# H3 convolution layers interleaved with ReLU MLPs on one core: a different early order, paired hidden buffers, two chunks kept in SBUF, and 70 extra small matmuls

## The chip, the core and the metric

The kernel runs on one core of a Trainium2 chip. Its engines are TensorE (PE in the profile; PEld is its weight load), VectorE (DVE), ScalarE (ACT), GpSimd (POOL) and SyncE (SP, which here issues nearly all transfers). Each works through its own list of instructions in the order in which the program put them, and waits where an operand isn't there. The metric is the device time of one execution in microseconds.

## What is computed

The input x (1 x 2048 x 640, float32) goes through four layers in turn, each with a residual: a gated long convolution (A), an MLP (B), and both again with the same weights.

```python
x = q
for _ in range(2):
    x = x + layernorm(x) * (longconv(shift(k) * v, ssm_k) + shift(k) * v * ssm_D)   # A
    x = x + relu(layernorm(x) @ w1) @ w2                                            # B
```

The convolution doesn't depend on x: it is one array Y (2048 x 640), used twice. shift is a causal convolution over 4 taps, longconv a causal one over all 2048 positions, per channel. w1 is 640 x 1728, w2 is 1728 x 640.

## The kernel before, in words

The 2048 rows are cut into 8 chunks of 256, and each chunk into two halves of 128 rows. The convolution works in a transformed domain: `transform` (line 356) makes the spectra of a chunk's inputs (`at`) and of its filter piece (`gt`), `products` (543) multiplies and adds them over all earlier chunks on VectorE (lines 583 to 587), transforms back and writes Y. Spectra that later chunks need go out to DRAM in `spills` (533) and come back through `get` (570) into a ring of four buffers, `ag`.

The MLP is made of float16 pairs. A float32 value is split into a high part and a low remainder, and a product is three matmuls: high by high, high by low, low by high. To split the weights they are first scaled by a power of two worked out from their norms. `norms` (672) loads the 14 tiles of w1 and then the 14 of w2 (320 KB each, line 682) and sums their squares on TensorE into `pw0` and `pw1` (line 689, five matmuls for each tile). A VectorE instruction takes the diagonal (694), a small matmul sums it (`pn`, 696), and a short chain of one-element instructions on VectorE and ScalarE (697 to 700) gives the scale `wsc`. `wsplit` (708) then makes of each of the 28 tiles a high part on ScalarE (716) and a low part on VectorE (717); tile 6 of w1 gets two small copies more (722).

`prep` (817) normalises a half or a whole chunk and brings it to TensorE's layout, `xT`, as a high and a low part. For the very first half this is done with transposes on TensorE (889) and copies by ScalarE (895) and VectorE (893); all others use DMA transposes (882). The first half's chain is: mean on VectorE (848), centred copy `xc` (850), squares on ScalarE (849), root (851), reciprocal `rstdB` on VectorE (852), high part `xh` on ScalarE (853), low part `xl` on VectorE (854).

`main` (898) is the MLP of one half or chunk. It goes through seven blocks of 256 hidden units in the order 0, 1, 2, 3, 6, 4, 5 (JS, line 30). `mm1` (994) gives a block's hidden values in one of two PSUM buffers `h`; ScalarE takes the ReLU as high part `hh` (1054, 1059), VectorE the remainder `hl` (1055, 1060), which frees the PSUM buffer; `mm2` (977) multiplies `hh` and `hl` with w2 into the sums `o` and `oc`. The rings of `hh` and `hl` hold two buffers each (NH). Block 6 is a half block and has one more matmul of its own (1067), which waits for a copy by ScalarE (`tb`, 1058). The first two chunks are worked on half by half (mains 0 to 7), the others whole. The last mains use a scheme with seven products for eight (line 942).

The order of all this isn't written out. Every operation is recorded with an engine, an assumed cost, what it reads and writes, and a class of urgency; `Plan.order` (129) then plays a list scheduler over them and fixes the order of each engine's list. For transfers it assumes a rate (DBW, line 49). So a change of one assumed number moves instructions on every engine. 50 small matmuls without use at the program's start (line 1162) are part of the kernel before.

Of the kernel before, what the change touches and what calls it, by code (L numbers as in the profile page):

```python
# [13 lines left out]
F16 = mybir.dt.float16  # L14
# [7 lines left out]
P = 128  # L22
S = 2048
# [3 lines left out]
NC = S // C  # L27
# [11 lines left out]
NSPIN = 50  # L39
BM = 1.7  # L40
CLS = (0, 1, 2.2, 2, 2.5, 3)
DDP = -6.5
CP = (-7, -6, -4.9)
WLAG = 3
POOLMOD = 5
CRIT, SLACK = -1, 0.6
PEOUT = 0.35
SAFE = 1.5
DBW, DLAT = 310e3, 1.9
LATE_DOWN = 0.0  # L50

# [10 lines left out]
AADD, RADD = (), ()  # L62
GADD, SADD = 4, 4
WINO = ((7, 0), (6, 1), (7, 1))
ONPOOL = ()

# [28 lines left out]
class Plan:  # L95
# [5 lines left out]
    def op(self, eng, cost, fn, reads=(), writes=(), prio=0, nbytes=0, late=0.0):  # L101
        o = Op()
        o.late = late
        o.eng, o.cost, o.fn, o.seq, o.nbytes = eng, cost, fn, len(self.ops), nbytes
        o.prio = (prio, o.seq)
        deps, o.new, o.outs = set(), [], []
        for t in reads:
# [21 lines left out]
    def order(self):  # L129
# [27 lines left out]
        while n < len(self.ops):  # L157
# [27 lines left out]
            for e in engs:  # L185
# [23 lines left out]
                if best.nbytes:  # L209
                    dma = max(dma, now + DLAT) + best.nbytes / DBW  # L210
                    end = dma + 1.1
# [26 lines left out]
def tile_h3_mlp(ctx: ExitStack, tc: tile.TileContext, q, kT, vT, shk, hF, hR, dD, w1, w2, cM, cG, out):  # L238
# [21 lines left out]
    def pe(cost, fn, reads, writes, prio, late=0.0):  # L260
        plan.op("PE", cost, fn, reads, writes, prio, late=late)
# [271 lines left out]
    def spills(u, at, gt, pr_):  # L533
        for i, (c, t) in enumerate(u):
            if c < NC - 2 or c == NC - 2 == u[-1][0]:
                dma(3072, lambda i=i, c=c, t=t: SP.dma_start(G_d[c][t].t, gt[:, i].rearrange("p a b c -> p (a b c)")), [gt], [G_d[c][t]], max(pr_, SPILL))
                dma(3072, lambda i=i, c=c, t=t: SP.dma_start(A_d[c][t].t, at[:, i].rearrange("p a b -> p (a b)")), [at], [A_d[c][t]], max(pr_, SPILL))

    Ysb = {}

    gate = Tile(None, [], F32, "gate")

    def products(u, at, gt, after):
# [18 lines left out]
        else:  # L562
            for i, (a, t) in enumerate(u):
                macs += [(i, c, a - c, t) for c in range(a + 1)]
        tl = {}
        for i, (c, t) in enumerate(u):
            tl["A", c, t] = (at, lambda i=i: at[:, i].rearrange("p a b -> p (a b)"))
            tl["G", c, t] = (gt, lambda i=i: gt[:, i].rearrange("p a b c -> p (a b c)"))

        def get(k, c, t):  # L570
# [101 lines left out]
    def norms():  # L672
# [3 lines left out]
        for k, e in ((0, 9), (1, 13)):  # L676
# [23 lines left out]
            dve(1, lambda pw=pw, sc=sc, e=e: DVE.tensor_scalar(sc.t, pw.t, -1.0, float((254 + e) << 23), op0=ALU.mult, op1=ALU.add), [pw], [sc], URGENT)  # L700
            out_.append((pw, sc))
        (p0, s0), (p1, s1) = out_
        inv = keep(const, [P, 1], "winv")
# [194 lines left out]
    def main(n, a, layer, S, xTS):  # L898
# [26 lines left out]
        fin = (a, layer) == (NC - 1, 1)  # L925
        plain = (NFP - 1, JS[-1]) if fin else (NFP - 1,)

# [94 lines left out]
        def second(j, *x):  # L1022
            if len(x) == 4:
                wprod(j, *x)
            else:
                wplain(j, *x)

        prev = None
# [169 lines left out]
    xTs = [prep(0, 0, (0,), CRIT)]  # L1198
    xTs.append(prep(0, 0, (1,), BACK))
    wsplit()  # L1200
    xT = xTs[0]
    cGs = csplit(cGt, 4, True, [WT[JS[-1], 1, 1]])
    for n, (a, l, S) in enumerate(order):
        nxt = xTs[1] if n == 0 else xT
        if n + 1 < len(order):
            na, nl, nS = order[n + 1]
            if n == 0 or nl == 0 and nS == (1,):
                pass
            elif nl == 0:
                conv_to(na)  # L1210
# [94 lines left out]
```

## Time and profile before

| what | value |
|---|---|
| time, median of 3 | 859.57 us (859.12 to 860.65) |
| the profiled execution | 859.22 us |
| its span, first to last instruction | 857.4 us |
| TensorE busy | 839.9 us, 7738 matmuls |
| VectorE busy | 743.4 us |
| ScalarE busy | 482.9 us |
| mean granted clock of TensorE | 0.995 |
| moved by DMA | 181.18 MB |

The 1.8 us between the span and the execution's time are outside the program's instructions. A row of the timeline holds the start, the duration, engine, line, operation, output and inputs of an instruction or of several equal ones, and in brackets how long its engine stood idle before it and what ended that. A row of the view by stretches holds the stretch, its length, then the busy time of PE, PEld, DVE, ACT and POOL with the number of instructions, the granted clock, the share of the DMA engines and GB/s.

### The profile page before, as it was taken

Reading aid. Unit: us, or ns where it says so; the run is one execution under the profiler, and the core shown is the slowest. Engines: PE = TensorE matmul, PEld = TensorE weight load, DVE = VectorE, ACT = ScalarE, POOL = GpSimd, SP = SyncE. Lnnn points to the kernel's source line nnn. Section 1 sums busy time; section 2 is a strip of 40 time slices with the busy share of each in tenths; the row PEclk is TensorE's granted clock in tenths of the full one; section 3 lists DMA queues with packets and bytes.
Section 4 is the critical chain, followed back from the end, with each engine's and each line's share of the span. In section 5 each row is a group of like instructions: output and inputs, shape, how many; then the busy total and the mean of one; then the engine's idle time right before and its main releaser. Section 6 shows DMA issues by size and latency. Waiting matters only on the chain.

```text
span 857.4 us, 19580 instructions
## 1 busy us (share of the span) xinstructions
PE 839.9 (98%) x7738; PEld 661.2 (77%) x7738; DVE 743.4 (87%) x1367; ACT 482.9 (56%) x1121; POOL 46.2 (5%) x57
## 2 busy tenths in 40 slices
PE   8789999999999999999999999999999999999997
PEld 8767788788878777777777777778777777888886
DVE  7999999999999999999999999999887758655543
ACT  6687586546586366738448283735416265737331
POOL 1000000000011001101011000011000000000000
PEclk9899999999999999999999999999999999999999
DMA  9886868998999969989898878597987663110200
GB/s 326 317 279 243 276 198 279 275 311 276 288 254 288 339 168 271 202 254 242 213 244 245 224 212 185 175 268 229 239 283 248 152 196 93 32 33 1 45 19 31
DMA packets 134989, 181.18 MB, mean 211 GB/s; under 512 B 50673, under 2 KB 87281, under 8 KB 134898
## 3 DMA queue, kind: packets, MB, share of 16 engines
q1 hardware_dynamic: 126578, 169.46, 64.0%
q0 software_dynamic: 8320, 10.49, 8.5%
q8 instruction: 60, 0.98, 0.5%
q14 instruction: 31, 0.25, 0.1%
HBM read 123.61 MB, written 35.65 MB: 186 GB/s over the span
## 4 chain that ended last, share of the span: by engine, by line
PE 85%; DVE 8%; ACT 4%; issue 1%; DMA 1%; SPq 0%; DVEq 0%; ACTq 0%
PE h L1015 12%; PE h L1018 12%; PE h L1016 12%; PE o L987 8%; PE o L988 8%; PE o L990 8%; PE o L942 7%; PE oc L987 2%; PE oc L988 2%; PE oc L990 2%; PE pg L466 1%; ACT w L716 1%; PE pq L609 1%; PE hb L1015 1%; PE hb L1016 1%
## 5 line engine op out<-in xcount | busy, mean ns | idle before, releaser
L1015 PE MATMUL h<-xT,w 128*128 128x256 f16 (+1 forms) x1290 | 301.5, 252 | 2.1 <-DVE hl L1060 1.9
L1018 PE MATMUL h<-xT,w 128*128 128x256 f16 (+1 forms) x1290 | 301.2, 251 | 0.0
L1016 PE MATMUL h<-xT,w 128*128 128x256 f16 (+1 forms) x1290 | 301.2, 251 | 0.0
L1016 PEld LDWEIGHTS <-w 128*128 128x128 f16 x1390 | 136.0, 98 | 14.1 <-issue 3.6
L1015 PEld LDWEIGHTS <-w 128*128 128x128 f16 x1390 | 136.1, 98 | 10.5
L988 PE MATMUL o<-w,hh 128*128 128x512 f16 x364 | 137.9, 379 | 0.4 <-DVE w L717 0.4
L987 PE MATMUL o<-w,hh 128*128 128x512 f16 x364 | 138.1, 379 | 0.0
L587 DVE TENSOR_TENSOR pacc<-pacc,pd 128x768 f32<-128x768 f32 x140 | 133.2, 952 | 0.8
L1018 PEld LDWEIGHTS <-w 128*128 128x128 f16 x1290 | 126.2, 98 | 8.9
L990 PE MATMUL o<-w,hl 128*128 128x512 f16 x338 | 128.1, 379 | 0.0
L1054 ACT ACTIVATE hh<-h 128x512 f16<-128x512 f32 (+1 forms) x103 | 50.6, 491 | 120.9 <-PE h L1018 119.7
L987 PEld LDWEIGHTS <-hh 128*128 128x128 f16 x728 | 71.2, 98 | 45.3 <-issue 1.0
L988 PEld LDWEIGHTS <-hh 128*128 128x128 f16 x728 | 71.3, 98 | 45.2
L990 PEld LDWEIGHTS <-hl 128*128 128x128 f16 x676 | 66.1, 98 | 40.5 <-issue 0.9
L586 DVE TENSOR_TENSOR pd<-Ax,Gx 128x768 f32<-128x768 f32 x87 | 81.7, 951 | 3.3 <-DMA Gx<-G 3.2
L987 PE MATMUL oc<-w,hh 128*128 128x128 f16 x364 | 79.7, 219 | 0.0
L988 PE MATMUL oc<-w,hh 128*128 128x128 f16 x364 | 79.7, 219 | 0.0
L990 PE MATMUL oc<-w,hl 128*128 128x128 f16 x338 | 74.0, 219 | 0.0
L1055 DVE SCALAR_TENSOR_TENSOR hl<-h,hh 128x512 f16<-128x512 f32 (+1 forms) x103 | 57.9, 562 | 12.0 <-ACT hh L1054 11.8
L389 ACT ACTIVATE tp<-kt,shs 128x256 f32<-128x256 f32 (+1 forms) x78 | 43.4, 574 | 20.3 <-DVE acc L426 20.3
L586 DVE TENSOR_TENSOR pd<-at,Gx 128x768 f32<-128x768 f32 x44 | 41.2, 952 | 0.5 <-DMA Gx<-G 0.5
L407 POOL DMA_DIRECT2D gs<-hr x20 | 19.0, 948 | 359.5 <-ACT tp L389 189.5
(225 smaller groups left out, 1556.4 us busy)
## 6 DMA issues: line engine op xcount, KB each, us to landing
Ax<-A SPq DMA_DIRECT2D x91, 384.0 KB, 4.5
Gx<-G SPq DMA_DIRECT2D x91, 384.0 KB, 4.6
G<-gt SPq DMA_DIRECT2D x32, 384.0 KB, 4.2
A<-at SPq DMA_DIRECT2D x32, 384.0 KB, 5.1
y<-Y SPq DMA_DIRECT2D x30, 320.0 KB, 4.2
ws<-in_w SPq DMA_DIRECT2D x28, 320.0 KB, 6.6
x<-in_q SPq DMA_DIRECT2D x16, 320.0 KB, 4.9
out_dram<-x SPq DMA_DIRECT2D x16, 320.0 KB, 2.7
```

What stands on the lines that cost most here:

```text
L389: ACT.activation(o[:, i : i + m], kview(i, m, j), AF.Copy, scale=shs[:, t, j : j + 1])
L586: ew(f"mac{j % POOLMOD}", 768, lambda e, pd=pd, av=av, gv=gv: e.tensor_mul(pd.t, av(), gv()), [ax, gx], [pd], pr_)
L587: dve(768, lambda i=i, pd=pd: DVE.tensor_add(acc[:, i], acc[:, i], pd.t), [acc, pd], [acc], pr_)
L942: PE.matmul(b[:, c : c + w], x, y[:, z : z + w], start=done[i] == 1, stop=done[i] == total[i])
L987: PE.matmul(z, hh[:, c], wh[:, d], start=(j == JS[0] and i == 0 and (h == 0 or s == S[0])), stop=False)
L988: PE.matmul(z, hh[:, c], wl[:, d], start=False, stop=end and tail)
L990: PE.matmul(z, hl[:, c], wh[:, d], start=False, stop=end)
L1015: PE.matmul(p[:, z], wh, xv(t, 0), start=b, stop=False)
L1016: PE.matmul(p[:, z], wh, xv(t, 1), start=False, stop=tail and e)
L1018: PE.matmul(p[:, z], wl, xv(t, 0), start=False, stop=e)
L1054: act(2 * R, lambda p=p, hh=hh: ACT.activation(hh.t, p.t, AF.Relu), [p], [hh], URGENT)
L1055: dve(2 * R, lambda p=p, hh=hh, hl=hl: DVE.scalar_tensor_tensor(hl.t, p.t, 0.0, hh.t, op0=ALU.max, op1=ALU.subtract), [p, hh], [hl], URGENT)
```

## The change

- The planner assumes 385 GB/s for transfers in its first 45 us and 310 GB/s after that, in place of 310 throughout.
- For the mains of a half chunk, `hh` and `hl` of a block share one buffer, and the blocks take it in turn from the ring that was for `hh` and the one that was for `hl`. A buffer is wide enough for both, so four blocks can be held at a time in place of two. The class `Part` stands for one of the two.
- 70 small matmuls (identity by identity, 128 x 128, float16) are recorded behind the norm of w1, with the lowest urgency. They read `s2`, that norm's sums, so that none starts ahead of it.
- The spectra of chunk 6 for the last two blocks of channels stay in their buffers for the products of chunk 7 (`held`) and are no longer stored and loaded again.
- Three edits name new constants that change no instruction: BK has the value of BM; EARLY asks for a main of a chunk ahead of the last, of the first layer, in the seven-product list, and there is none; and `conv_to(NC)` reaches the same units as `conv_to(7)`.

The diff, cut to its core (a plus is the changed kernel):

```diff
+NWARM = 70
+DBW0, FIRST = 385e3, 45
+PAIRED = 1
...
-                    dma = max(dma, now + DLAT) + best.nbytes / DBW
+                    dma = max(dma, now + DLAT) + best.nbytes / (DBW0 if now < FIRST else DBW)
...
-            if c < NC - 2 or c == NC - 2 == u[-1][0]:
+            if c < NC - 2:
...
-        tl = {}
+        tl = dict(held)
...
+        if u[0][0] == NC - 2 == u[-1][0]:
+            held.update(tl)
...
+            if k == 0 and NWARM:
+                spin2 = T(ps, "h", 2, [P, 512], "spin2", stream=2)
+                for _ in range(NWARM):
+                    pe(0.057, lambda spin2=spin2: PE.matmul(spin2[:, 0:P], ident16.t, ident16.t, start=True, stop=True), [ident16, s2], [spin2], IDLE)
...
-                hh = T(mlp, "hh", NH, [P, 2 * R], f"hh{n}_{j}", F16, stream=sm)
-                hl = T(mlp, "hl", NH, [P, 2 * R], f"hl{n}_{j}", F16, stream=sm)
+                if len(S) == 1 and PAIRED:
+                    both_parts = T(mlp, ("hh", "hl")[JS.index(j) % 2], NH, [P, 2, 2 * R], f"hh{n}_{j}", F16, stream=sm)
+                    hh, hl = (Part(both_parts, k) for k in range(2))
+                else:
+                    hh = T(mlp, "hh", NH, [P, 2 * R], f"hh{n}_{j}", F16, stream=sm)
+                    hl = T(mlp, "hl", NH, [P, 2 * R], f"hl{n}_{j}", F16, stream=sm)
```

What the planner makes of it, in the order of the changed program's lists up to the end of main 0:

- SP: the first tiles of w1 go among the last inputs of chunk 0: one ahead of `kt`, one ahead of `vt`, two ahead of `hf`, where before two stood behind `vt` and none earlier. The last tile of w2 waits for no engine any more, only for its place in the queue. The DMA transposes for main 1 come eleven places later. From the end of chunk 6 on, four stores and four loads of 384 KB are gone.
- PE: `pn0` stands behind 45 of the 70 matmuls into `pw1` (ten before). The other 25, in fives, have 52 small matmuls among and behind them: 3, 10, 10, 10 and 19; then `pn1`, 18 small ones, both groups of transposes, and only then the first product of main 0. Before, the transposes and the first product stood among the last 25. Main 0 then runs `mm1` of blocks 0 to 3, and from there on takes `mm1` of block 6 (both halves) and of block 4, further ahead of `mm2` than before, and three halves of `mm1` of main 1 (one before) ahead of the last product of main 0.
- DVE: the diagonal of `pw1` stands ahead of `rstdB`, and the first low part of a weight behind both (before, that low part stood ahead of `rstdB` and the diagonal eleven places behind it).
- ACT: the ReLU of block 6 stands ahead of the splits of block 4 of w1 (before, behind those, behind two splits of w2 and behind both of block 5).

More of the change, by code (lines that the diff above doesn't have):

```diff
@@ L39 @@
 NSPIN = 50
-BM = 1.7
+BM, BK = 1.7, 1.7
 CLS = (0, 1, 2.2, 2, 2.5, 3)
@@ L63 @@
 GADD, SADD = 4, 4
+PAIRED = 1
 WINO = ((7, 0), (6, 1), (7, 1))
+EARLY = 3
 ONPOOL = ()
@@ L105, in op @@
         o.prio = (prio, o.seq)
+        reads, writes = ([getattr(t, "tile", t) for t in x] for x in (reads, writes))
         deps, o.new, o.outs = set(), [], []
@@ L539, in tile_h3_mlp @@
     Ysb = {}
+    held = {}
     gate = Tile(None, [], F32, "gate")
@@ L925, in main @@
         fin = (a, layer) == (NC - 1, 1)
-        plain = (NFP - 1, JS[-1]) if fin else (NFP - 1,)
+        plain = (NFP - 1, JS[-1]) if fin else (NFP - 1, *JS[:EARLY]) if wino and a < NC - 1 and layer == 0 else (NFP - 1,)
         total, done = [0] * 6, [0] * 6
@@ L1026, in second, with __init__, t, __getitem__ @@
                 wplain(j, *x)
+        class Part:
+            def __init__(self, tile, k):
+                self.tile, self.k = tile, k
+            @property
+            def t(self):
+                return self.tile.t[:, self.k]
+            def __getitem__(self, i):
+                return self.t[i]
         prev = None
@@ L1198, in tile_h3_mlp @@
     xTs = [prep(0, 0, (0,), CRIT)]
-    xTs.append(prep(0, 0, (1,), BACK))
+    xTs.append(prep(0, 0, (1,), BK))
     wsplit()
@@ L1209, in tile_h3_mlp @@
             elif nl == 0:
-                conv_to(na)
+                conv_to(NC if WINO and (na, nl) == WINO[0] else na)
                 if WINO and (na, nl) == WINO[0]:
```

## The prediction

> **What bounds the kernel now.** First the view by stretches, cut where TensorE's waits change (columns: PE, PEld, DVE, ACT, POOL busy, granted clock, DMA share, GB/s):
>
> ```profile
> 34.00:36.00 2.00, 0.43 (x8) 0.25 (x5) 2.00 (x11) 1.85 (x3) 0.00 (x0) 1.00 0.48 178
> 36.00:38.00 2.00, 0.00 (x0) 0.00 (x0) 1.64 (x4) 1.97 (x5) 0.00 (x0) 0.63 0.26 42
> 38.00:40.00 2.00, 1.41 (x12) 1.25 (x13) 2.00 (x3) 1.91 (x4) 0.00 (x0) 0.50 0.94 342
> 40.00:42.00 2.00, 2.00 (x21) 2.00 (x20) 1.46 (x3) 1.76 (x3) 0.00 (x0) 0.50 0.97 216
> 42.00:44.00 2.00, 2.00 (x27) 2.00 (x25) 2.00 (x5) 1.11 (x2) 0.00 (x0) 0.66 1.03 341
> 44.00:62.00 18.00, 14.77 (x176) 11.56 (x173) 16.88 (x38) 16.05 (x33) 0.00 (x0) 1.00 0.85 258
> 62.00:75.47 13.47, 13.39 (x170) 10.66 (x170) 13.34 (x29) 10.69 (x21) 0.00 (x0) 1.00 0.77 287
> 75.47:150.00 74.53, 74.46 (x805) 59.92 (x803) 71.65 (x146) 52.21 (x138) 0.00 (x0) 1.00 0.77 247
> 150.00:250.00 100.00, 98.59 (x1103) 78.91 (x1101) 95.89 (x177) 60.15 (x147) 4.85 (x5) 1.00 0.94 279
> 250.00:848.00 598.00, 598.00 (x5128) 463.25 (x5127) 502.64 (x878) 315.88 (x726) 37.16 (x35) 1.00 0.68 186
> ```
>
> From 62 us on TensorE stands still for 1.6 us in all until 848, and what follows 848 is the last main's residual, which the change leaves alone. So the time is the moment at which TensorE runs on for good, plus the matmuls left. The half clock lasts from 36.5 (0.63 over two us) to 43.4 (0.66). Next, the view of waits and of VectorE's weight splits:
>
> ```profile
> PE xt L889 <- ACT xh L853: 3.9, 1, 3.9
> PE h L1015 <- DVE hl L1060: 1.9, 1, 1.9
> PE hb L1015 <- DVE hl L1055: 0.8, 1, 0.8
> SPq L682 <- DVE w L717: 5.9, 1, 5.9
> L716 ACT ACTIVATE w<-ws,wsc x28: 812/819/829, 34.2 to 68.8; 128x640 f16<-128x640 f32 x28
> L717 DVE SCALAR_TENSOR_TENSOR w<-ws,wsc,w x28: 867/880/885, 35.6 to 70.4; 128x640 f16<-128x640 f32 x28
> ```
>
> The small matmuls fill the first wait. But from 44 to 62 VectorE (16.88 of 18) and ScalarE (16.05) are nearly full, splitting weights, and TensorE waits for them again. So a first product that starts sooner or runs faster is lost again unless TensorE has other work while they split. Therefore I follow VectorE, not TensorE, through the new order.
>
> **The change part by part.** Rows that price the head, from the timeline:
>
> ```profile
> 32.12 0.28 PE L696 MATMUL pn<-ws,ones 128*128 128x1 f32 x2
> 32.26 2.17 PE L689 MATMUL pw<-ws 128*128 128x128 bf16 x35
> 38.33 0.71 PE L889 MATMUL xt<-ident,xh 128*128 128x128 f16 x5 [3.90 <-ACT xh L853]
> 40.11 0.31 PE L1005 MATMUL h<-xT,w 128*128 128x128 f16 x1
> 40.22 0.31 PE L1003 MATMUL h<-xT,w 128*128 128x128 f16 x1
> 44.57 0.22 PE L1015 MATMUL h<-xT,w 128*128 128x128 f16 x1
> 44.63 0.22 PE L1016 MATMUL h<-xT,w 128*128 128x128 f16 x1
> 32.89 0.15 DVE L697 TENSOR_SCALAR wn<-pn 128x1 f32<-128x1 f32 x1
> 33.97 0.15 DVE L700 TENSOR_SCALAR wsc<-wpw 128x1 int32<-128x1 int32 x1
> 36.87 0.16 DVE L852 RECIPROCAL rstdB<-stdB 128x1 f32<-128x1 f32 x1 [0.36 <-ACT stdB L851]
> 28.00:30.00 2.00, 2.00 (x30) 1.80 (x28) 1.99 (x8) 0.39 (x1) 0.00 (x0) 1.00 1.04 396
> ```
>
> *Two new waits of VectorE.* `pn0` now stands behind 45 matmuls into `pw1`. In the trace the first 45 end at 34.43 (ten earlier, then the row with 35), held back by the ninth tile of w2; transfers run at 396 GB/s, 0.83 us for a tile, so nothing brings it sooner. `pn0` goes from 32.12 to 34.25, and `wn` behind it from 32.89 to 34.6: 1.7 us late. All of VectorE's list waits behind `wn`. `wsc` follows 1.1 us later, at 35.7, and the mean, a sum of `gt` that the new order puts here (0.35) and `xc` end at 37.2. Then comes the diagonal of `pw1`, ahead of `rstdB`: it needs the 14th tile of w2. Before, SP held that load back by 5.9 us until a buffer was free; in the changed program it only queues, so the tiles behind the ninth (matmuls at 34.0) come every 0.83 us, and the last one's matmuls at 38.0 to 38.3. Diagonal at 38.5, `rstdB` at 38.85: 2.0 us later than before.
>
> *70 small matmuls.* Until the 14th tile they fill gaps: ten at 0.056 us (rows 44.57, 44.63) and five into `pw1` are 0.85 us, as long as a tile takes to come. Behind it stand 19, then `pn1`, then 18: 38.3 + 1.06 + 0.25 + 1.0 = 40.6. `xh` would be ready at 39.75 (ScalarE from 39.0), so they delay the first transposes by 0.85. But the second transposes need `xl`, which VectorE ends at 41.5 (low parts of two weights at 0.80, then 0.79), and both groups now stand ahead of the first product. It starts at 41.9 in place of 39.84, at full clock; it waits for the copy of `xT`'s low part until 42.85, and 20 matmuls later, at 43.97, block 0 is done. Before, that was at 44.57. So the small matmuls cost nothing at the bound as long as they hold the clock. What the clock is worth lies between nothing, if VectorE hides it all, and half of the 5.0 us from 38.33 to 43.4, 2.5 us (rows 40.11 and 40.22: 0.11 for a matmul of 0.056); I take nothing beyond the start times above.
>
> [...]
>
> *VectorE from `rstdB` to the blocks of main 0.* Its spacing, from the timeline:
>
> ```profile
> 52.35 0.42 DVE L1055 SCALAR_TENSOR_TENSOR hl<-h,hh 128x256 f16<-128x256 f32 x1
> 52.68 0.88 DVE L854 SCALAR_TENSOR_TENSOR xl<-xc,rstdB,xh 128x640 f16<-128x640 f32 x1
> 53.47 1.67 DVE L717 SCALAR_TENSOR_TENSOR w<-ws,wsc,w 128x640 f16<-128x640 f32 x2
> 55.07 0.68 DVE L411 TENSOR_TENSOR gs<-hf,hr 128x512 f32<-128x512 f32 x1
> 55.67 1.68 DVE L717 SCALAR_TENSOR_TENSOR w<-ws,wsc,w 128x640 f16<-128x640 f32 x2
> 59.84 1.68 DVE L717 SCALAR_TENSOR_TENSOR w<-ws,wsc,w 128x640 f16<-128x640 f32 x2
> 61.74 0.29 DVE L1060 SCALAR_TENSOR_TENSOR hl<-h,hh 128x128 f16<-128x128 f32 x1 [0.21 <-ACT hh L1059]
> 62.08 0.22 PE L1015 MATMUL h<-xT,w 128*128 128x128 f16 x1 [1.87 <-DVE hl L1060]
> ```
>
> From `rstdB` to the low part of block 5 of w1 the new list has 20 weights (0.80 each, 16.0), five `hl` (0.34, 1.7), two `xl` (0.79, 1.6), two `gs` and one sum of the same size (0.60, 1.8), and a copy, a centring and a dozen small ones (together about 1.75): 22.85. Waits for ScalarE, which runs the high parts just ahead, add 0.6 by the same counting on its list (mainly block 2). That gives 38.85 + 23.45 = 62.3. In the trace it was 59.84 + 1.6 = 61.44, so the splitting is 0.9 us later than before.
>
> *What the new order and the paired buffers give back.* In the trace TensorE waits until 62.08 to begin block 4: its PSUM buffer is freed by block 6's `hl`, done at 62.0, whose `hh` came late in ScalarE's list. In the new list that `hh` stands ahead of the splits of block 4, at 55.2, and its `hl` at 55.5; block 4 runs when its weights are split, 58.15 to 59.8, and with four buffers for `hh` and `hl` it needs no second product to be over first. TensorE then does two products of block 2 and stands until block 5's weight at 62.3. From there every operand comes ahead of TensorE. Lengths:
>
> ```profile
> 48.16 0.22 PE L1015 MATMUL h<-xT,w 128*128 128x128 f16 x1
> 49.83 0.38 PE L987 MATMUL o<-w,hh 128*128 128x512 f16 x1
> 50.65 0.38 PE L987 MATMUL o<-w,hh 128*128 128x512 f16 x1
> xT<-xl SPq DMA_TRANSPOSE x1, 5.1
> ```
>
> A block's `mm1` is 1.67 (30 matmuls from 48.16 to 49.83), half of an `mm2` 0.82. Left at 62.08 in the trace, up to the end of the second block of main 1 (75.47), are 13.4 us. Left at 62.35 in the new order, up to the same set of work, are block 5 (1.67), `mm2` of blocks 3, 6, 4, 5 (1.64, 1.37, 1.64, 1.64), two blocks of main 1 (3.34) and four transposes of the convolution (0.44): 11.75, the difference being block 4. So TensorE is there at 74.1 in place of 75.47: **1.35 us gained**.
>
> *Chunk 6 kept in SBUF.* Eight transfers of 384 KB less, near 600 to 690 us. TensorE is full there (598.00 of 598), so I take 0; without that cover eight issues on SP, at about a transfer's 1 us each, bound it at 8 us of queue, of which none reaches TensorE today. The two spectra buffers held longer could cost as little.
>
> *DMA transposes for main 1* stand eleven places later on SP, behind a load that waits for VectorE's `gs` (53.9 in the new order). A transpose took up to 5.1 us (last row above); they land by 62.5, and main 1 first needs them at 66.5. Hidden; without the 4 us of slack each us late costs one.
>
> Sum: 859.22 - 1.35 = **857.9** (span 856.05 + 1.8). The profiled execution lies 0.35 under the median 859.57.
>
> **The rivals.** *Given back later: 859.2.* VectorE is 96% busy from 75 to 250 (71.65 of 74.53, 95.89 of 100) with the convolution, and it is no earlier than before when the splits end. If a chunk's convolution is what TensorE must wait for there, the 1.35 us come back as waits. For it: the waits of 1.5 us that exist there. Against: 7 us of VectorE idle in the same stretch.
>
> *Slower: the clock falls all the same, 859.8.* TensorE's fill from 33 to 36.5 is only about two thirds, since three small matmuls stand in the first gap. At half clock the 37 small ones behind the last tile take 4.0 in place of 2.1 us; `pn1` then holds VectorE's list up too, and the transposes come at 42.6. All of the 1.9 us reaches the first product and the splits behind its `hl`. It decides from 1.35 us of delay on: with less the kernel is still faster. A last tile of w2 that lands later than 37.6 works the same way, one for one, since VectorE waits in order for its diagonal; if it came as late as before, 1.9 us on, that too gives 859.8, and both together 861.7.
>
> *More: 856.5.* The new order also removes the waits of TensorE from 150 to 250 (100 - 98.59 = 1.4 us), or VectorE's two new waits are shorter than counted by as much.
>
> *It doesn't do what it says*: the small matmuls shift nothing, and only the order acts; that is the forecast's own time, as they are hidden in it.
>
> **How the numbers follow.** About 0.2% (1.7 us) is what a measurement of this kernel can tell from no change, so the forecast stands at that limit. Chances: forecast, 857.9 within 1 us either way, 0.48; given back 0.17; slower, 859.8 to 861.7, 0.18; more 0.17. The range leaves out a tenth at each side: below, the far end of the last case, above, most of the two together; the clock's upper bound of 2.5 us is in it as far as VectorE lets it through. It is 855.8 to 860.4. Against the median, faster by over 0.2% is under 857.85: half of the forecast's case and all of the last, 0.41. Slower by over 0.2% is over 861.3: half of the slower case, 0.09. Within: 0.50.
>
> **What would show it.** Granted clock 1.00 from 30 to 60. `pn0` near 34.25, `rstdB` near 38.85, first product near 41.9, block 5's second weight near 62.3, TensorE without a wait from there to 75. Wrong would be: a clock of 0.50 anywhere from 36 to 43; the last `pw1` matmuls later than 39; a wait of over 1 us on TensorE between 75 and 250 that wasn't there; a wait at main 1's first product for the DMA transposes.

## The result: 862.12 us, slower by a third of a per cent, and the profile after

| | before | changed |
|---|---|---|
| median, 9 runs each, same chip | 859.96 us (859.12 to 862.10) | 862.12 us (859.62 to 867.43) |
| ratio | | 1.0034, 95% interval 1.0018 to 1.0050 |
| the profiled execution | 859.22 us | 860.13 us |
| its span | 857.4 us | 858.4 us |

The forecast was 857.9, the range 855.8 to 860.4; the median lies above both. Two things are to be kept apart: the profiled execution is 0.9 us slower than that of before (it lies inside the range, 2.2 us above the forecast), and the other executions lie from 0.5 us below it to 7.3 us above. On three further chips (runs e5, e16 and e18 below) the same program gave 1.0009, 1.0012 and 1.0019; e5's interval includes 1.

The view by stretches of the changed kernel, cut as before (columns: stretch, length, busy time of PE, PEld, DVE, ACT, POOL with instructions, granted clock, DMA share, GB/s):

```profile
36.00:38.00 2.00, 1.50 (x27) 1.33 (x25) 1.30 (x7) 1.97 (x5) 0.00 (x0) 1.00 1.03 380
38.00:40.00 2.00, 2.00 (x39) 2.00 (x36) 1.06 (x4) 1.28 (x2) 0.00 (x0) 1.00 1.09 356
...
44.00:62.00 18.00, 16.39 (x200) 12.73 (x198) 17.42 (x31) 17.93 (x37) 0.00 (x0) 1.00 1.02 327
62.00:75.47 13.47, 12.84 (x149) 9.34 (x147) 13.40 (x26) 10.13 (x18) 0.00 (x0) 1.00 0.18 51
75.47:150.00 74.53, 74.10 (x808) 59.59 (x807) 72.00 (x150) 50.74 (x130) 0.00 (x0) 1.00 0.81 249
150.00:250.00 100.00, 97.82 (x1087) 78.57 (x1087) 93.19 (x174) 61.04 (x155) 6.05 (x6) 1.00 0.92 279
250.00:848.00 598.00, 598.00 (x5124) 462.69 (x5123) 505.27 (x883) 316.15 (x726) 36.07 (x34) 1.00 0.66 181
```

The half clock is gone (1.00 where 0.63 and 0.50 stood), and from 44 to 62 TensorE is 1.6 us busier (16.39 after 14.77). So the early edits do what they say. But from 75.47 to 250 TensorE now stands still for 2.6 us (0.43 + 2.18) instead of 1.5, although VectorE is no busier there. The view of TensorE's waits names the places (columns: waiting instruction, releaser, us in total, times, longest). Where VectorE writes `hh` in the changed kernel's rows, it is the remainder that was called `hl`, since the shared buffer has one name:

```profile
PE pg L471 <- ACT at L521: 1.2, 1, 1.2
PE hb L1099 <- ACT tb L1090: 1.0, 2, 0.6
PE o L1005 <- DVE hh L1087: 0.9, 1, 0.9
...
PE xt L904 <- DVE wpw L709: 0.6, 1, 0.6
PE h L1033 <- DVE w L732: 0.4, 1, 0.4
```

The first is at 175.5 us and the third at 169.0; before had neither. The rows of the timeline that answer to the forecast's steps, and after them the start of the last first-product matmul of three cuts (block 1 of main 1, main 4, main 15):

```profile
34.27 0.33 PE L706 MATMUL pn<-ws,ones 128*128 128x1 f32 x2
38.94 0.29 DVE L704 SCALAR_TENSOR_TENSOR dg<-pw,ident 128x128 f32<-128x128 f32 x1 [1.64 <-PE pw L699]
39.16 0.16 DVE L867 RECIPROCAL rstdB<-stdB 128x1 f32<-128x1 f32 x1
42.00 0.45 PE L904 MATMUL xt<-ident,xl 128*128 128x128 f16 x5 [0.56 <-DVE wpw L709]
42.29 0.22 PE L1018 MATMUL h<-xT,w 128*128 128x128 f16 x1
63.36 0.23 PE L1033 MATMUL h<-xT,w 128*128 128x128 f16 x1 [0.45 <-DVE w L732]
74.32 0.22 PE L1033 MATMUL h<-xT,w 128*128 128x128 f16 x1
193.09 0.22 PE L1033 MATMUL h<-xT,w 128*128 128x128 f16 x1
672.33 0.27 PE L1033 MATMUL h<-xT,w 128*128 128x256 f16 x1
```

The same three cuts of the kernel before:

```profile
75.42 0.22 PE L1018 MATMUL h<-xT,w 128*128 128x128 f16 x1
192.16 0.22 PE L1018 MATMUL h<-xT,w 128*128 128x128 f16 x1
671.59 0.27 PE L1018 MATMUL h<-xT,w 128*128 128x256 f16 x1
```

At the first cut the changed kernel is 1.10 us ahead, but four transposes of the convolution (0.43 us) that before had done by then still stand behind it, so its true lead is 0.67 us. At main 4, with the same work done in both, it is 0.93 us behind. At main 15 it is still 0.74 behind. **The lead is lost, and 0.9 us more, in the convolution's stage between the first cut and main 4.** Next to nothing (0.2 us, behind main 15) is lost after 250 us in this execution.

### The profile page after: what moved, and what is told of

It reads as the page before. It is cut to its first block, busy times and chain, and to the rows that moved or that the text cites. A ratio compares the mean times of both kernels' runs of the same rounds, so it can differ in the third digit from the quotient of the medians.

```text
span 858.4 us, 19690 instructions
## 1 busy us (share of the span) xinstructions
PE 843.4 (98%) x7808; PEld 663.1 (77%) x7808; DVE 743.1 (87%) x1367; ACT 482.2 (56%) x1121; POOL 46.5 (5%) x57
## 4 chain that ended last, share of the span: by engine, by line
PE 81%; DVE 10%; DMA 4%; ACT 3%; issue 2%; SPq 1%; DVEq 0%; ACTq 0%
PE h L1030 12%; PE h L1033 12%; PE h L1031 12%; PE o L1003 8%; PE o L1002 8%; PE o L1005 7%; PE o L957 7%; PE oc L1003 2%; PE oc L1002 2%; PE oc L1005 2%; DMA A<-at 1%; PE pq L619 1%; DVE pd L596 1%; PE hb L1030 1%; PE hb L1031 1%
## 5 line engine op out<-in xcount | busy, mean ns | idle before, releaser
L1005 PE MATMUL o<-w,hl 128*128 128x512 f16 x234 | 88.7, 379 | 0.0
L596 DVE TENSOR_TENSOR pd<-Ax,Gx 128x768 f32<-128x768 f32 x83 | 77.8, 951 | 0.9 <-DMA Gx<-G 0.8
L1005 PEld LDWEIGHTS <-hl 128*128 128x128 f16 x468 | 45.8, 98 | 27.6
L1005 PE MATMUL oc<-w,hl 128*128 128x128 f16 x234 | 51.2, 219 | 0.0
L1087 DVE SCALAR_TENSOR_TENSOR hl<-h,hh 128x512 f16<-128x512 f32 x55 | 37.6, 685 | 11.0 <-ACT hh L1086 11.0
L596 DVE TENSOR_TENSOR pd<-at,Gx 128x768 f32<-128x768 f32 x46 | 43.2, 951 | 0.6 <-DMA Gx<-G 0.5
```

The source lines that it names most:

```text
L596: ew(f"mac{j % POOLMOD}", 768, lambda e, pd=pd, av=av, gv=gv: e.tensor_mul(pd.t, av(), gv()), [ax, gx], [pd], pr_)
L1005: PE.matmul(z, hl[:, c], wh[:, d], start=False, stop=end)
L1087: dve(2 * R, lambda p=p, hh=hh, hl=hl: DVE.scalar_tensor_tensor(hl.t, p.t, 0.0, hh.t, op0=ALU.max, op1=ALU.subtract), [p, hh], [hl], URGENT)
```

## Experiments: who takes the lead away

Which edit moves which order was read from the lists of instructions. The small matmuls shift nothing on any engine: with or without them the lists are the same, in either order. Keeping chunk 6 changes the lists from about 566 us on only. The new rate replans nearly everything from the first microseconds on (the first difference on SP's queue comes at 8 us), the paired buffers from 48 us on. So the runs can hold the order fixed and change one thing in it.

All were timed beside the kernel before on the same chip. "Lead" is the time of before minus that of the run at the cut named, equal work taken into account (0.43 to 0.45 us off at the first two cuts in the new order, nothing from main 4 on); it comes from one execution of each, against the 859.22 us execution of before. Mains are counted from 0 here; "main 5" in the texts of e6, e7 and e9 is main 4 of this table.

| run | order | median us | ratio (95%) | lead: block 1 of main 1 | main 2 | main 4 | main 6 | main 15 |
|---|---|---|---|---|---|---|---|---|
| changed, first result | new | 862.12 | 1.0034 (1.0018 to 1.0050) | 0.67 | 0.89 | -0.93 | -0.70 | -0.74 |
| e5 changed again | new | 860.97 | 1.0009 (0.9998 to 1.0021) | 0.39 | 0.62 | -0.82 | -0.58 | -2.68 |
| e16 changed, third | new | 860.55 | 1.0012 (1.0001 to 1.0023) | 1.06 | 1.28 | -0.02 | 0.19 | -0.17 |
| e18 changed, fourth | new | 860.69 | 1.0019 (1.0010 to 1.0027) | 0.41 | 0.63 | -1.49 | -1.27 | -1.29 |
| e1 no small matmuls | new | 860.16 | 0.9999 (0.9989 to 1.0009) | -0.10 | 0.12 | -1.07 | -1.03 | -1.17 |
| e17 the same again | new | 860.92 | 1.0013 (1.0004 to 1.0021) | 0.44 | 0.65 | -0.18 | -0.38 | -1.74 |
| e7 less convolution, early | new | 860.41 | 1.0008 (0.9994 to 1.0022) | 0.59 | 0.82 | -1.21 | -0.98 | -1.00 |
| e9 less convolution, late | new | 861.22 | 1.0015 (1.0003 to 1.0027) | 0.83 | 1.05 | -0.07 | 0.18 | 0.15 |
| e6 kt ahead of stores | new | 860.06 | 0.9999 (0.9988 to 1.0011) | 1.29 | 1.51 | 0.40 | -0.10 | -0.90 |
| e10 stores by GpSimd | new | 859.91 | 1.0000 (0.9991 to 1.0009) | 1.37 | 1.60 | 0.19 | -0.19 | -1.06 |
| e13 hr later | new | 860.21 | 1.0003 (0.9994 to 1.0011) | 1.22 | 1.44 | -0.79 | -0.56 | -0.59 |
| e14 stores and hr | new | 859.90 | 1.0003 (0.9994 to 1.0011) | 0.47 | 0.69 | 0.25 | -0.03 | -0.05 |
| e2 small matmuls alone | old | 858.88 | 0.9985 (0.9975 to 0.9996) | 1.07 | 1.01 | 0.32 | 0.32 | 0.31 |
| e12 the same again | old | 858.96 | 0.9988 (0.9980 to 0.9997) | 0.41 | 0.21 | 0.19 | 0.19 | 0.19 |
| e8 small and chunk 6 kept | old | 859.50 | 0.9994 (0.9983 to 1.0004) | 0.11 | 0.11 | 0.10 | 0.11 | 0.11 |
| e11 small, stores by GpSimd | old | 858.10 | 0.9979 (0.9970 to 0.9987) | 0.97 | 0.97 | 0.96 | 0.96 | 0.96 |
| e15 stores by GpSimd only | old | 859.13 | 0.9990 (0.9980 to 1.0000) | -0.73 | -1.49 | -1.49 | -1.50 | -1.51 |

Read it along the rows: in the new order every run is ahead, or level, at main 2, and has lost between 0.7 and 2.0 us of that by main 6. In the old order e8 and e11 keep what they have up to main 15, e11 to the hundredth; e12 loses 0.2 us of it, e2 0.7 us. One execution need not stand for the median: the profiled ones of the first result, e16 and e9 were 2.0, 1.0 and 2.0 us faster than their medians, those of e5 and e15 1.1 and 1.3 us slower (e15's the slowest of its eleven).

### One edit out, one edit alone

**e1_no_small**, and again as **e17_no_small_again** beside the changed kernel (e18):

```diff
-NWARM = 70
+NWARM = 0
```

> The changed kernel without its 70 small matmuls; every other instruction stands in the same order on every engine. Theory A (the front gains about 1.1 us as the profile of the changed kernel shows, block 1 of main 1 done at 74.3 in place of 75.4, and the loss is made later, between 140 and 180 us, by the new order of the convolution): the granted clock falls to 0.5 somewhere from 36 to 44, the first transposes start up to 1 us sooner, VectorE's splits end as before within 0.5 us, block 1 of main 1 at 74.0 to 75.0; the median stays within 1 us of the changed kernel's 862.1 and the runs scatter as much (some over 864). Theory B (the small matmuls themselves cost, through the list of TensorE and through VectorE's wait for the second norm): 859.5 to 860.2 and little scatter.

> The changed kernel without its 70 small matmuls, all else in the same order, beside the changed kernel on the same chip. If the small matmuls are worth in the new order what they are in the old (0.12 to 0.15%), this one is about 1 us slower than the next run. If the new order gives their gain back (150 to 176), the two are within 0.6 us, with less scatter of the clock in the next. If they cost something there (they stand ahead of the first transposes), this one is faster by 0.6 us or more.

> The changed kernel unaltered, beside the run without small matmuls. Expected: ratio 1.0005 to 1.002; TensorE waits near 168 and 175 as before.

Without the small matmuls the clock falls again, as before the change: it is 0.50 from 38 to 44 us in e1, and its mean over an execution is 0.992 to 0.998 in e1 and 0.993 to 0.997 in e17, against 0.998 to 1.000 in e18. e1's 860.16 us lies in the range of its theory B (the small matmuls cost), but the changed kernel did not run on its chip; on the chip of e17 and e18 the two take 860.92 and 860.69 us: in the new order the small matmuls make no difference that can be told. **e2_small_alone**, and again as **e12_small_again**, leaves them as the only edit:

```diff
-DBW0, FIRST = 385e3, 45
+DBW0, FIRST = 310e3, 45
-PAIRED = 1
+PAIRED = 0
...
-            if c < NC - 2:
+            if c < NC - 2 or c == NC - 2 == u[-1][0]:
...
-        if u[0][0] == NC - 2 == u[-1][0]:
-            held.update(tl)
```

> The kernel before with the 70 small matmuls and nothing else changed; every other instruction stands in the order of before. Theory A: the clock stays at 1.00, block 0 of main 0 is done up to 1 us sooner, but VectorE and ScalarE set the pace until 62 us, so block 1 of main 1 at 75.0 to 75.5 (75.4 before) and the time 859.4 to 860.2, within 0.5 us of before, with little scatter. Theory B: 861 to 862.

> The kernel before with only the 70 small matmuls, a second time and on this chip. First time: 0.9985 (0.9975 to 0.9996). Expected 0.998 to 0.9995, with a clock of 1.00 from 36 to 44.

There they gain 0.12 to 0.15%, 0.8 to 0.9 us, twice, more than e2's text had expected (within 0.5 us of before). So the part that was to cost nothing and gain nothing is the part that gains, and the new order is what loses. Its two causes one by one, **e3_pairs_alone** (`PAIRED = 1` alone) and **e4_rate_alone** (`DBW0 = 385e3` alone), both without small matmuls:

> The kernel before with the paired buffers for hh and hl alone (planned anew, the head up to block 3 of main 0 as before). Theory A: block 4 no longer waits until 62, so block 1 of main 1 is done 1 to 2 us sooner (73.5 to 74.5); what the order from 75 to 250 does with it is open: 858 to 859 if the waits there stay at 2.4 us, 860 to 863 if the order there is the trouble. Theory C (the pairing itself costs): block 1 of main 1 no sooner than 75.4.

> The kernel before with the planner's 385 GB/s for the first 45 us alone: the head of the changed kernel, without small matmuls and with two buffers for hh and hl. Theory A: VectorE's two new waits are there (pn0 near 34.3, rstdB near 39), nothing gives the lost time back, and block 1 of main 1 comes at 75.4 to 76.5; total 859.5 to 862 by what the later order adds.

They took 866.71 us (ratio 1.0069, 1.0049 to 1.0088) and 869.72 us (1.0117, 1.0097 to 1.0137), both far above what was expected of them (at most 863 and 862). Both lose most of it late: 5.8 and 8.0 us between the ends of mains 11 and 12. TensorE's wait there and the stretch from 475 to 500 us, first e3, then e4:

```profile
PE h L1028 <- DMA xT<-xh: 3.5, 1, 3.5
...
475.00:500.00 25.00, 21.18 (x161) 14.93 (x159) 24.52 (x37) 11.25 (x27) 0.91 (x1) 0.93 0.91 236
```

```profile
PE h L1028 <- DMA xT<-xh: 5.5, 1, 5.5
...
475.00:500.00 25.00, 19.36 (x146) 14.02 (x145) 22.66 (x34) 10.50 (x24) 2.08 (x2) 0.86 0.95 250
```

A DMA transpose for a whole chunk's main arrives late, some 430 us after the edit acted, and in the stretch with the wait the mean clock is 0.93 and 0.86. The changed kernel, with both edits, has no such wait (25.00 us busy from 475 to 500, at a clock of 1.00). Nor is its own late load (next section) in these two orders: there `kt` goes out at 161.34 and 160.33 us. An early edit thus draws a different late order each time, and what it draws weighs more than what it does early. **e8_small_and_held** is e2 with the spectra of chunk 6 kept:

> The kernel before with the 70 small matmuls and with the spectra of chunk 6 kept, without the new rate and the paired buffers: the early order is that of the kernel before. The small matmuls alone gave a ratio of 0.9985. If keeping the spectra is worth nothing, as TensorE is full there, the ratio is the same within 0.05%: 0.998 to 0.999. If the order that it changes near the end costs something, the ratio is 0.9995 or more and TensorE waits past 600 us.

0.9994, no better than without. The intervals overlap with those of e2 and e12 (0.9985 and 0.9988), but its profile shows a wait of TensorE at 704.9 us, past 600 us, that before, e2 and e12 don't have:

```profile
PE hb L1030 <- DVE hl L1087: 0.6, 1, 0.6
```

It is 0.11 us ahead at main 15 and 0.7 us behind at the end. So the order that this edit draws near the end may well cost something in the old program; in the changed kernel's profile only 0.2 us go there, without a wait.

### Amount of work or late loads

ScalarE's wait for `kt`, a load of chunk 3's taps, is 4.4 us in the changed kernel. SP's and ScalarE's rows, first the kernel before:

```profile
152.06 0.38 SPq L375 DMA_DIRECT2D hf<-in_hF  x1
160.45 0.53 SPq L375 DMA_DIRECT2D kt<-in_kT  x1
162.06 2.30 SPq L650 DMA_DIRECT2D Y<-ys  x4
165.04 0.51 ACT L389 ACTIVATE acc<-kt,shs 128x256 f32<-128x256 f32 x1 [1.31 <-DMA kt<-in_kT]
```

and the changed kernel:

```profile
155.12 0.38 SPq L380 DMA_DIRECT2D hf<-in_hF  x1
163.69 1.96 SPq L660 DMA_DIRECT2D Y<-ys  x4
166.70 0.38 SPq L380 DMA_DIRECT2D kt<-in_kT  x1
172.50 0.51 ACT L394 ACTIVATE acc<-kt,shs 128x256 f32<-128x256 f32 x1 [4.38 <-DMA kt<-in_kT]
174.91 0.57 ACT L521 ACTIVATE at<-pr 128x512 f32<-128x512 f32 x1
```

SP issues `hf` 3.1 us later (it waits 4.6 us for VectorE's `gs`, 1.7 before), and four stores of Y have moved ahead of `kt`, which goes out 6.25 us later. From its issue to ScalarE's row the load takes 5.8 us, 4.6 before. ScalarE stands behind it in order, so `at` ends late and TensorE's `pg` at 175.5 waits for it. Theory 1: late loads make the loss. Theory 2 (the forecast's own rival): VectorE's amount of convolution does. **e5_changed_again** is the base on this chip. **e6_kt_ahead_of_stores** moves only the four stores:

```diff
         out, end = self.order()
+        names = lambda o: [t.name for t in o.tiles]
+        ys = [o for o in out if o.eng == "SP" and "ys2_0" in names(o)]
+        out = [o for o in out if o not in ys]
+        k = next(i for i, o in enumerate(out) if o.eng == "SP" and "kt3_1" in names(o))
+        out[k + 1 : k + 1] = ys
```

> The changed kernel, unaltered, beside the others of this batch. If its loss lies in its order (loads and stores of the convolution that SP issues later, 150 to 176 us), the profile shows the same waits again, ScalarE some 4 us for the load of kt near 172 and TensorE about 1 us near 169 and near 175, and the time is 860 to 863. If the loss of the first runs was a matter of that chip, the time is within 0.1% of the kernel before. If a transfer late in the convolution (475 to 500) goes wrong now and then, the times scatter by several us and the profile may show a wait there of 3 us or more.

> The changed kernel with one thing moved: the four stores of Y for chunks 2 and 3 stand on SP behind the two loads of spectra and the load of kt for the next two chunks, as they do in the kernel before, not ahead of them. All else is in the same order on every engine. Theory 1, the loads come late because SP waits for those stores' operand: kt is issued near 164.5 in place of 166.7, ScalarE's wait near 172 falls from 4.4 to about 2, TensorE's wait of 1.2 near 175.5 goes, and the last product of main 5 ends 1 to 2 us sooner than in the changed kernel: 858.5 to 859.5 by profile. Theory 2, VectorE's amount of work from 75 to 176 sets the pace: ScalarE's wait is shorter but VectorE is late all the same and the time is that of the changed kernel within 0.4 us.

**e7_less_convolution** and **e9_less_before_gs** leave out two multiply-add pairs each (in e9 the tuple is (5, 6)); the unit "2_0" is the first block of channels of chunks 2 and 3, so Y is incomplete there in both chunks, not in chunk 2 alone:

```diff
+            out_ = nm == "2_0" and j in (2, 3)
-            ew(f"mac{j % POOLMOD}", 768, lambda e, pd=pd, av=av, gv=gv: e.tensor_mul(pd.t, av(), gv()), [ax, gx], [pd], pr_)
+            ew(f"mac{j % POOLMOD}", 768, lambda e, pd=pd, av=av, gv=gv, out_=out_: out_ or e.tensor_mul(pd.t, av(), gv()), [ax, gx], [pd], pr_)
-            dve(768, lambda i=i, pd=pd: DVE.tensor_add(acc[:, i], acc[:, i], pd.t), [acc, pd], [acc], pr_)
+            dve(768, lambda i=i, pd=pd, out_=out_: out_ or DVE.tensor_add(acc[:, i], acc[:, i], pd.t), [acc, pd], [acc], pr_)
```

> The changed kernel without two of the multiply-add pairs on VectorE for the first two channel blocks of chunk 2 (four instructions of 0.95 us, near 126 to 134 us; Y of chunk 2 is incomplete in those channels). All else is in the same order on every engine, and no transfer goes. Theory 2, VectorE's amount of work sets the pace up to 176: its 3.8 us reach TensorE in good part, the last product of main 5 ends 1.5 to 2.5 us sooner than in the changed kernel, and the time is 857.5 to 858.7 by profile. Theory 1, late loads and stores set it: VectorE waits longer for the same loads, and the time changes by less than 0.5 us.

> The changed kernel without two other multiply-add pairs on VectorE, the last two of chunk 2's first channel blocks (3.8 us, near 148 to 152 us; Y of chunk 2 is incomplete in those channels). Order and transfers are unchanged. Theory 1a, a chain of VectorE and SP sets the pace: the sums gs end near 155, they release the load of hf, and SP then issues without a gap until kt at 166.7. With VectorE's list shorter just ahead of gs, hf, the transposes and kt are issued 2 to 3.5 us sooner, ScalarE's wait for kt near 172 falls below 2.5 us, TensorE's wait near 175.5 falls below 0.5 and main 5's last first product ends 1 us or more sooner than 193.0. Theory 1b, only SP's own queue, full from earlier on: kt is issued within 1 us of 166.7 and nothing changes.

Two stretches, 125 to 150 and 150 to 175, of e5 and then of e7:

```profile
125.00:150.00 25.00, 25.00 (x287) 20.24 (x286) 24.82 (x47) 18.02 (x49) 0.00 (x0) 1.00 0.89 280
150.00:175.00 25.00, 23.16 (x251) 18.61 (x249) 23.34 (x40) 12.18 (x32) 0.00 (x0) 1.00 0.79 237
```

```profile
125.00:150.00 25.00, 25.00 (x288) 20.34 (x287) 21.88 (x43) 17.98 (x50) 0.00 (x0) 1.00 0.89 281
150.00:175.00 25.00, 22.96 (x249) 18.41 (x247) 22.92 (x39) 11.62 (x30) 0.00 (x0) 1.00 0.80 232
```

VectorE has 2.9 us less to do in the first stretch (third busy column, 24.82 to 21.88) and TensorE gains nothing; it waits longer in the second (23.16 to 22.96). `kt` is issued at 166.63 against 166.75. Theory 2 has fallen for the work up to 150. In e9 `hf` goes out only 0.7 us sooner (153.82 against 154.51 in e5) and `kt` at 166.25: the 2 to 3.5 us expected of a chain from VectorE's `gs` did not come either, and its median, 861.22, is no better. VectorE waits 2.0 and 1.3 us for ScalarE there instead (at 149.1 and 151.6). Now e6:

```profile
164.82 0.39 SPq L385 DMA_DIRECT2D kt<-in_kT  x1
165.25 1.89 SPq L665 DMA_DIRECT2D Y<-ys  x4
169.76 0.51 ACT L399 ACTIVATE acc<-kt,shs 128x256 f32<-128x256 f32 x1 [2.14 <-DMA kt<-in_kT]
```

`kt` goes out 1.9 us sooner than in e5, ScalarE's wait falls from 4.58 to 2.14, and TensorE's wait of 1.7 us at 175 is down to 0.3, as theory 1 had it. But the gain doesn't last, and the time by profile, 860.27, is not the 858.5 to 859.5 of theory 1. TensorE's waits from 150 to 250, e5's wait at 175 first and then e6's:

```profile
PE pg L471 <- ACT at L521: 1.7, 1, 1.7
...
PE o L1010 <- DVE hh L1092: 0.9, 1, 0.9
PE o L1010 <- DVE sums L1190: 0.8, 1, 0.8
PE pg L476 <- DVE gs L421: 0.3, 1, 0.3
```

The first of e6's (168.5) was there in e5 (0.6), the second (201.6) is new: TensorE comes there sooner, and the remainder of the ReLU that it needs stands behind the convolution's work in VectorE's list. Ratio 0.9999 against 1.0009; the intervals overlap. **e10_stores_by_gpsimd** goes further and takes all 42 stores of that stage off SP:

```diff
         for o in out:
+            self.onpool = o.eng == "SP" and 75 < o.start < 200 and not o.new and re.match(r"[AGY]\d", o.tiles[-1].name) is not None
...
+    class Issuer:
+        def __getattr__(self, name):
+            return getattr(POOL if plan.onpool else nc.sync, name)
+
+    SP = Issuer()
```

> The changed kernel with 42 stores (spectra A and G and the results Y, those planned between 75 and 200 us) issued by GpSimd, which has nothing to do there, in place of SP; all else is in the same order. Theory 1, SP's queue makes the loads late: from the load of hf to the load of kt SP issues 3 us less and kt is issued near 163.5, ScalarE's wait near 172 is under 2 us, TensorE's waits from 150 to 180 fall from 2.2 to under 1, and the ratio to the kernel before falls from 1.0009 to 0.999 or less. If VectorE's work alone sets the stage, it stays within 0.04% of 1.0009. If stores issued by GpSimd hold back the loads in the transfer engines, or GpSimd takes longer to issue and ys and at come free late, it is slower.

`kt` at 165.4, ScalarE's wait 2.8, no wait at 175, but TensorE waits at 148, 150, 169 and 201.7 (0.7, 0.6, 0.9 and 0.7 us by the view of waits). Ratio 1.0000: about what e6 gave, short of what was expected. The same edit on e2 is **e11_small_stores_by_gpsimd**, and on the kernel before **e15_stores_by_gpsimd_only**:

> The kernel before with the 70 small matmuls and with its stores between 75 and 200 us issued by GpSimd. The small matmuls alone gained 1.07 us in front and kept 0.3 by profile. If the rest was lost to SP's queue, it comes back: ratio 0.9970 to 0.9980. If not, the ratio is that of the next run within 0.05%.

> The kernel before with nothing changed but its stores between 75 and 200 us, issued by GpSimd. If SP's queue costs only what TensorE gains ahead of it, the ratio is 1.000 (0.9993 to 1.0005) and the 0.9979 of small matmuls and stores together is a gain that neither gives alone. If the queue holds the kernel before back by itself, the ratio is 0.9992 or less.

e11's rows:

```profile
159.27 0.91 SPq L388 DMA_DIRECT2D kt<-in_kT  x1
164.44 0.51 ACT L402 ACTIVATE acc<-kt,shs 128x256 f32<-128x256 f32 x1 [1.67 <-DMA kt<-in_kT]
161.00 1.60 POOL L666 DMA_DIRECT2D Y<-ys  x3 [0.40 <-DVE ys L658]
```

**e11 is the fastest version here: 858.10 us, ratio 0.9979 (0.9970 to 0.9987), faster than both kernels**, with its ten executions from 857.82 to 858.84. Its lead of 0.97 us runs through unchanged to main 15. With the stores on SP, e2, e12 and e8 end at 0.31, 0.19 and 0.11 there, whatever they led by in front; e2 lost 0.7 of 1.07 us, most of it in a wait at 168.8 (0.5 us). Of the two outcomes named for e15 the second came: 0.9990 (0.9980 to 1.0000), so SP's queue may hold the kernel before back as well, and the gains of e12 and e15 add up to about that of e11.

### The scatter

In e5's profile 2.1 us more are lost between the ends of mains 8 and 9. Its rows there, and the row of before:

```profile
336.47 0.63 ACT L411 ACTIVATE hr<-hr 128x512 f32<-128x512 f32 x1 [5.72 <-DMA gs<-hr]
337.64 0.39 PE L1002 MATMUL o<-w,hh 128*128 128x512 f16 x1 [0.63 <-ACT hh L1086]
```

```profile
333.66 0.62 ACT L406 ACTIVATE hr<-hr 128x512 f32<-128x512 f32 x1
```

`hr` may be turned only when the adding transfer that reads it has landed. In the new order ScalarE comes to it 3.1 to 5.7 us too soon (3.46, 5.72, 3.98 and 3.08 in the four profiles of the changed kernel) and a ReLU stands behind it; in the kernel before it doesn't wait. At 3.5 us TensorE doesn't feel it, at 5.7 it loses 2.1 us. In between lie other profiles of the same order, e16 and e10:

```profile
333.95 0.63 ACT L411 ACTIVATE hr<-hr 128x512 f32<-128x512 f32 x1 [3.98 <-DMA gs<-hr]
334.62 0.63 ACT L419 ACTIVATE hr<-hr 128x512 f32<-128x512 f32 x1 [4.26 <-DMA gs<-hr]
```

From the last first-product matmul of main 6 (249.6 us in the first profile) to one near 389.7 us, e16 loses 0.34 us against the first profile and e10 0.63; e6, with a wait of 4.04, loses 0.41, and the profiles with 3.6 us and less (e1, e7, e9, e17, e18) lose nothing. In these executions what the wait has beyond some 3.64 us reached TensorE one for one, in e5 too (5.72 less 3.64 is 2.08, and 2.1 were lost). **e13_hr_later** moves it, **e14_both_places** does this and e10's edit, with **e16_changed_third** as the base:

```diff
         out, end = self.order()
+        names = lambda o: [t.name for t in o.tiles]
+        late = [o for o in out if (o.eng, names(o)) in (("ACT", ["hr4_3"]), ("POOL", ["hr4_3", "gs14_3"]))]
+        out = [o for o in out if o not in late]
+        k = next(i for i, o in enumerate(out) if o.eng == "ACT" and "hh9_1" in names(o))
+        out[k + 1 : k + 1] = late
```

> The changed kernel with one instruction of ScalarE, the copy of hr with its sign turned (near 334 us), and the transfer on GpSimd that follows it, moved three products of ScalarE later, behind the ReLU of block 1 of main 9. All else is in the same order. If ScalarE's wait there for a transfer (3.5 us in one profile, 5.7 in another, nothing in the kernel before) is what makes the slow executions, TensorE has no wait from 320 to 375, and the times scatter less: highest under 861.8, median 0.3 to 1 us under that of the unaltered changed kernel in the same batch. If the scatter comes from elsewhere (150 to 176), median and highest stay within 0.3 us of it.

> The changed kernel with the stores of 75 to 200 us issued by GpSimd and with hr moved, both places mended at once. If these two places are the whole of the loss, what the early stages gain is kept: ratio to the kernel before 0.9980 to 0.9992. If other waits of the new order take over (VectorE's list near 149, 169 and 201), it is 0.9993 to 1.0005, and the small matmuls in the old order remain the better kernel.

> The changed kernel unaltered, a third profile. Expected: ratio 1.0005 to 1.003, the waits near 169 and 175 again, ScalarE's wait at hr between 3 and 6 us, and the loss against the kernel before of 2 to 3 us between the ends of main 3 and main 4 once more.

e13: 859.82 to 861.26, against 859.53 to 863.92 for the unaltered kernel, and the median 0.34 us lower: the spread shrinks as expected if the wait at `hr` makes the slow executions. (The spread is read from a dozen executions each; e17, which has the wait, also stayed within 859.85 to 861.49. And e17's profile loses 1.3 us in another place, between 440 and 560 us, with waits for a DMA transpose and for VectorE of 0.3 and 0.6 us.) e14, with both places mended, is at 1.0003 (0.9994 to 1.0011), level with the kernel before but not ahead: other waits of the new order, near 150, 169 and 201 in its trace, take 0.7 of its lead between main 2 and main 6 (0.69 to -0.03).

## Why the prediction was wrong, step by step

**Head: right.** `pn0` 34.25 forecast, 34.27 measured; `rstdB` 38.85 and 39.16; clock 1.00 from 30 on. `rstdB` is 0.31 late because the last matmuls into `pw1` let the diagonal start at 38.94 in place of 38.5. The first product came at 42.3, not 41.9: the second transposes waited 0.56 us for VectorE, whose `xl` ended at 41.95 in place of 41.5. The rival of a falling clock did not occur.

**The early gain: right mechanism, half the size.** 1.35 us forecast; 0.67 measured, 0.39, 1.06 and 0.41 in three other executions. The mis-sized term is block 5's second weight: 62.3 forecast, 63.36 by TensorE's row. Of the 1.06 us, 0.31 are `rstdB`'s and about 0.7 VectorE's list behind it (24.1 us to that weight in place of 23.45). TensorE had 11 of block 5's matmuls behind it by then, which returns some of it, and waited once more for a weight at 64.2.

**The small matmuls: priced at nothing beyond the start times.** That was wrong in the old order, where they alone gain 0.8 to 0.9 us (e2, e12), and right in the new one, where e17 and e18 end level. That the order there gives the gain back is likely, not shown: at main 2 the runs with the small matmuls lead by 0.62 to 1.60 us, e1 and e17 by 0.12 and 0.65, and by main 6 the difference is gone.

**The step that failed: "From there every operand comes ahead of TensorE."** The lists had been followed to the end of main 0; behind it the old trace was taken to go on, shifted. But the new rate and the paired buffers replan all that follows, and there a load goes out 6.25 us later and a copy on ScalarE comes before its transfer. The text named the sign to watch, a wait of over 1 us between 75 and 250 that wasn't there; it came, 1.2 us at 175.5 (1.7 in e5), and with it 0.9 us for VectorE at 169.0.

**The rival "given back later" had the place right, the size wrong, and the cause at most in part.** It let only the 1.35 us come back, through VectorE's amount of work. e7 shows that taking 2.9 us of that work away up to 150 changes nothing, though the waits at 169 and 201 are still for VectorE; and the loss does not stop at what had been gained: it belongs to the new order, with or without the early gain (e1, e17). So the range ended too low.

**The DMA transposes of main 1: right,** no wait of main 1 for them in the trace. **Chunk 6: no gain, as forecast; no cost only in the changed kernel's profile.** In e8 the same edit comes with a wait of 0.6 us and a loss of 0.8 us behind main 15, so taking 0 because TensorE is full there left out what the edit does to the order. (What is kept are two blocks of channels of one chunk, not two chunks as the title says.)

**What is shown, and what stays open.** Shown: the loss lies between main 2 and main 6 in the new order; one of its waits there is SP's late `kt`, down to 0.3 us when the stores stand behind it (e6); a further loss in some executions is ScalarE's early `hr`, gone when it is moved (e13). Open: the waits for VectorE's list near 150, 169 and 201, for which no run took the cause away; why `kt` goes out at 166.0 to 167.9 in the unmended new order whatever TensorE's lead; and why the first chip gave 1.0034 where three others gave 1.0009 to 1.0019.

## What to carry to other kernels

Where a planner makes the order, an edit of one assumed number is a new program from that point on: follow the new lists of every queue to the end, SP's and the copies that wait for a transfer above all, or take the time as unknown by some us either way. Separate first what leaves all lists the same (here the small matmuls) from what redraws them, and measure each alone. Here the gain ahead of the convolution's stage was kept whole in e11 (0.97 us, and 0.96 at main 15), where `kt` went out 1.2 us sooner than before (159.27 after 160.45), and lost in the changed kernel (0.67 to -0.74), where it went out 6.25 us later. That the loads alone decide it is not shown, since e6 and e10, which issue `kt` 1.3 to 1.9 us sooner than e5, lost their lead to other waits; but look at which queue issues the loads of a stage and what stands ahead of them there.

## What the runs showed of the hardware

The mean granted clock of the kernel before is not the same in every execution. In the batch of e9 most of its 34 executions fall into groups by it: 17 at 0.995 with a median of 860.04 us, 10 at 0.997 with 859.34, one each at 0.994 with 860.88 and at 0.993 with 862.48; the other five (three at 0.996 with 858.79 to 859.06, two at 0.998 with 859.48 and 861.37) don't follow that order in their times, so the clock is not all that moves them. From 0.997 to 0.995 the step in time is 0.70 us. Why the clock differs between executions of one kernel no run here shows.

A store issued by GpSimd takes it about as long as one takes SP: 1.60 us for three (e11) against 1.96 for four (the changed kernel), so about 0.5 us each. Here, where SP issues nearly all transfers and GpSimd issued nothing else from 75 to 200 us, the same stores from GpSimd came with the better time (858.10 against 858.96 on one chip, e11 and e12; the intervals of the ratios, 0.9970 to 0.9987 and 0.9980 to 0.9997, overlap).
